# Batch 0's key copies from twin PSUM tiles, its values pooled ahead of late scores, and other slots for the attention steps, in a fused pooled-attention and maxout-FFN kernel

## The chip, the cores and the metric

One core of a Trainium2 chip. Times are device microseconds of one execution; medians of several executions, with their range, are quoted. A ratio is the mean time of one kernel's fast runs over that of the other's in the same rounds, so it is not quite the ratio of the quoted medians; beside it stands a 95% interval. A trace is one execution under the profiler, and its span lies some 1.7 us below that execution's time. The experiments ran in three batches of rounds on three chips, each beside the kernel before (medians 269.27, 269.48 and 269.42 us) but not beside the changed kernel. A comparison with the changed kernel therefore goes across batches, and by the intervals of the ratios its error is some 0.7 to 0.9 us.

## The reference, cut to what matters

```python
k_p = k.reshape(B, H, Sp, pool, D).mean(axis=3)      # (B, H, S, D) = (8, 8, 576, 64)
v_p = v.reshape(B, H, Sp, pool, D).mean(axis=3)      # pool 8, so Sp = 72
scores = scale * np.matmul(q, k_p.transpose(0, 1, 3, 2))
scores = scores - np.max(scores, axis=-1, keepdims=True)
attn = np.exp(scores)
attn = attn / (np.sum(attn, axis=-1, keepdims=True) + 1e-09)
x = np.matmul(attn, v_p)                             # then (B*S, H*D) = (4608, 512)
h = np.maximum(np.maximum(x @ w1, x @ w2), x @ w3)   # (4608, 768)
out = h @ w_out                                      # (4608, 512), float32
```

The FFN is most of the work. It runs in nine blocks of 512 tokens, and a batch has 576. So block n multiplies tokens of batches up to n, and the attention of batch n + 1 is put between its matmuls.

## The kernel before: the parts that the change and the argument touch

Names in the code and the traces: `pkp` is the pooled keys in PSUM and `kp` their copy, `pkt` their transpose and `kz` its copy; `pqt` and `qT` are the same for queries. `psc` is scores and `et` their exponentials, `pvp` and `vp` pooled values, `pav` attention times values, `xn` the same normalised, `pxt` and `xT` its transpose and the copy of that. `pw`, `t` and `hT` belong to the FFN's hidden layer, `po` and `osb` to its output, and `wm` is a warm-up matmul, whose result nobody reads. A timeline line gives start, duration, engine, line, operation and count; a bracket is the idle time of the engine before it and what ended that.

A generator yields after each piece of work, and the instruction order of every engine is the order in which the pieces are emitted. A "part" below is one yield of the FFN: four matmuls `pw` and one evacuation, 0.87 us on TensorE at full width. "Slot 5" is the place behind part 5 of a block.

```python
TR = ("tr", 1)     # PSUM tag and number of buffers: one
PW = ("pw", 3)     # FFN accumulators: three; tag "att" has two

def turn_k(b, evacs, tag):               # pooled keys, transposed, into the masked key tile
    pkt = psp.tile([128, 6, 96], BF16, name="pkt", tag=tag[0], bufs=tag[1])
    for i in range(6):
        nc.tensor.transpose(pkt[:, i, :], kps[b][:, i, :, :], ident[0:96, 0:96])
    for par in range(2):
        rows = slice(64 * par, 64 * par + 64)
        evacs[par](out=kz_all[b % 2][rows, par, :, 0:Sp]..., in_=pkt[rows]...)

def queries(b):                          # 4 query steps, keys after the third, 8 scores
    for m, (n0, n1) in enumerate(((0, 5), (5, 10), (10, 14), (14, 18))):
        turn_q(b, n0, n1, nc.scalar.copy, TR)
        yield
        if m == 2 and b > 1:
            turn_k(b, V_V, TR)           # both copies by VectorE
            yield
    for h in range(H):
        scores(b, h)                     # TensorE, then exp on ScalarE
        yield

def outputs(b, tags=(TR,) * 5):          # values, normalise (VectorE), transpose, copy (ScalarE)
    last = None
    for (c0, keep), tag in zip(CHUNKS, tags):
        xn = values(b, c0)
        yield
        if last:
            turn_x(*last)
            yield
        last = (b, c0, keep, xn, tag)
    turn_x(*last)
    yield

def hidden_part(n, jc, c0, c1, hT):      # one part per weight
    for wi in range(3):
        ...                              # pw: 4 matmuls, tag "pw"
        # wi 0: ScalarE copies pw to t;  wi 1: VectorE max(t, pw);  wi 2: VectorE max -> hT
        yield

# ... start of batch 0: one pooled-key tile, copied by VectorE and then ScalarE
def spread(i0, i1):
    nc.vector.tensor_copy(out=kps[0][:, i0:i1, 0, :], in_=pkp0[0:96, i0:i1])
    nc.scalar.copy(out=kps[0][:, i0:i1, 1, :], in_=pkp0[0:96, i0:i1])
# ... turn_k, turn_q, turn_q; scores4(0); turn_q, turn_q; scores4(4); scores2(0);
#     pool_v; scores2(2); pool_v; scores2(4); pool_v; scores2(6); then values, outputs

# ... blocks 1 to 8: slot of each of the 23 steps of batch n + 1; the rest is drained at the end
PLAN = (1, 2, 4, 5, 7, 8, 9, 10, 11, 12, 13, 14, 15, 16, 17, 17, 18, 18, 19, 19, 20, 20, 21)
PLAN1 = (7, 8, 10, 13, ...)              # block 1, whose first parts have half width
```

The softmax here doesn't subtract the row's maximum and nothing guards it: scores larger than these inputs give would overflow.

## Time and profile before

| | before |
|---|---|
| time, 3 runs | 269.28 us (269.11 to 269.28) |
| span of the trace | 267.3 us |
| first FFN matmul | 20.83 us |
| block 0 (20.83 to 54.04), block 1 (to 84.21) | 33.2 and 30.2 us |
| blocks 2 to 6, with attention | 27.36 us each |
| blocks 7 and 8, FFN alone | 20.7 us each |

The blocks are read off TensorE's timeline as the distance from the first `pw` of one to the first of the next. The lines that carry this are in the prediction.

### The profile page before, as it was taken

The numbers are of one execution on the slowest core, as the hardware profiler recorded it, in microseconds if no ns is written. First come the engines' busy times: TensorE is split into PE (matmuls) and PEld (weight loads), VectorE is DVE, ScalarE is ACT, GpSimd is POOL, SyncE is SP. The second block draws the span as 40 slices with busy tenths as digits, with TensorE's granted clock in tenths as the row PEclk, the third lists the DMA queues.
The fourth block names the chain that finished last, engine by engine and source line by source line (L and its number), as shares of the span: only waits on it lengthen the run. The fifth ranks groups of instructions, "written<-read, shape, count | busy, mean of one in ns | idle before, by whom it ended". The sixth has DMA issues, their size and how long they took to land.

```text
span 267.3 us, 4638 instructions
## 1 busy us (share of the span) xinstructions
PE 250.4 (94%) x1858; PEld 139.6 (52%) x1860; DVE 128.1 (48%) x227; ACT 132.9 (50%) x232; POOL 117.7 (44%) x84
## 2 busy tenths in 40 slices
PE   7598998998998999999999999999999999999993
PEld 2477546574555455545555555545554554444441
DVE  3447562555453646363645464455536464433440
ACT  1374248553755474547465655465555653223221
POOL 8662002999899999859970895000000000000000
PEclk9999999999999999999999999999999999999998
DMA  7999999698757958969777604200330033006006
GB/s 188 201 198 205 202 244 211 168 245 180 178 121 180 285 126 184 256 202 174 178 156 221 94 0 105 54 0 2 85 76 0 0 81 79 0 22 139 0 2 156
DMA packets 20866, 34.71 MB, mean 130 GB/s; under 512 B 2636, under 2 KB 13260, under 8 KB 20268
## 3 DMA queue, kind: packets, MB, share of 16 engines
q0 software_dynamic: 14048, 21.44, 41.1%
q1 hardware_dynamic: 6796, 12.98, 19.3%
q8 instruction: 14, 0.23, 0.4%
q14 instruction: 8, 0.07, 0.1%
HBM read 34.60 MB, written 9.44 MB: 165 GB/s over the span
## 4 chain that ended last, share of the span: by engine, by line
PE 83%; DVE 9%; ACT 5%; issue 1%; DVEq 0%; ACTq 0%
PE pw L267 45%; PE po L297 17%; PE psc L188 6%; PE pxt L208 4%; PE pqt L159 3%; DVE kz L169 3%; PE pav L217 3%; PE wm L316 3%; ACT et L193 2%; DVE xn L225 2%; DVE t L275 2%; ACT t L272 1%; PE pvp L148 1%; DVE hT L278 1%; ACT qT L161 1%
## 5 line engine op out<-in xcount | busy, mean ns | idle before, releaser
L267 PE MATMUL pw<-xT,mw 128*128 128x512 f16 (+1 forms) x696 | 157.2, 364 | 0.9 <-ACT xT L212 0.7
L267 PEld LDWEIGHTS <-mw 128*128 128x128 f16 x696 | 62.2, 98 | 50.9 <-issue 1.2
L275 DVE TENSOR_TENSOR t<-t,pw 128x512 f16<-128x512 f16 (+1 forms) x58 | 37.8, 651 | 79.0 <-PE pw L267 48.4
L272 ACT CAST t<-pw 128x512 f16<-128x512 f32 (+1 forms) x58 | 32.3, 557 | 43.2 <-PE pw L267 42.6
L297 PE MATMUL po<-mwo,hT 128*128 128x512 f16 x216 | 51.5, 379 | 0.0
L193 ACT ACTIVATE et<-psc 72x576 f16<-72x576 f32 (+2 forms) x62 | 40.5, 662 | 13.0 <-PE psc L188 12.9
L278 DVE TENSOR_TENSOR hT<-t,pw 128x512 f16<-128x512 f16 (+1 forms) x58 | 37.7, 650 | 15.4 <-PE pw L267 13.4
L127 POOL TENSOR_TENSOR vt<-vt 72x2048 f32<-72x2048 f32 (+1 forms) x12 | 41.2, 3434 | 2.6 <-DMA vt<-in_v_dram 2.1
L127 POOL TENSOR_TENSOR kt<-kt 96x1536 f32<-96x1536 f32 (+1 forms) x12 | 31.5, 2624 | 22.7 <-DMA kt<-in_k_dram 22.1
L301 ACT COPY osb<-po 128x512 f32<-128x512 f32 x36 | 21.1, 586 | 30.5 <-PE po L297 30.5
L297 PEld LDWEIGHTS <-hT 128*128 128x128 f16 x216 | 19.8, 98 | 18.9 <-DVE hT L278 0.4
L212 ACT COPY xT<-pxt 128x512 f16<-128x512 f16 (+1 forms) x40 | 21.8, 545 | 14.3 <-PE pxt L208 14.3
L225 DVE TENSOR_TENSOR xn<-pav,rcp 128x512 f16<-128x512 f32 x40 | 27.7, 692 | 1.4
L188 PE MATMUL psc<-qT,kz 128*128 128x64 bf16 (+3 forms) x192 | 25.4, 246 | 3.1 <-ACT qT L161 1.7
L161 ACT COPY qT<-pqt 128x640 bf16<-128x640 bf16 (+1 forms) x29 | 18.6, 641 | 18.1 <-PE pqt L159 18.1
L188 PEld LDWEIGHTS <-kz 128*128 128x128 bf16 x192 | 18.1, 98 | 17.5 <-issue 2.9
L217 PEld LDWEIGHTS <-et 72*128 72x128 f16 x320 | 15.7, 98 | 8.2 <-issue 0.6
L223 DVE RECIPROCAL rcp<-pav 128x8 f32<-128x8 f32 x40 | 8.1, 204 | 23.1 <-PE pav L217 23.1
L208 PE MATMUL pxt<-identh,xn 128*128 128x128 f16 x160 | 15.5, 219 | 2.3 <-DVE xn L225 2.1
L217 PE MATMUL pav<-vp,et 72*128 72x65 f16 x320 | 17.1, 194 | 0.4 <-ACT et L193 0.3
L159 PEld LDWEIGHTS <-qb 128*128 128x128 bf16 x144 | 9.9, 97 | 11.4 <-DVE kz L169 5.3
L159 PE MATMUL pqt<-ident,qb 128*128 128x128 bf16 x144 | 13.0, 219 | 2.7 <-DVE kz L169 2.3
(41 smaller groups left out, 107.9 us busy)
## 6 DMA issues: line engine op xcount, KB each, us to landing
out_dram<-osb SPq DMA_DIRECT2D x72, 128.0 KB, 2.4
kt<-in_k_dram POOLq DMA_DIRECT2D x5, 1152.0 KB, 7.6
vt<-in_v_dram POOLq DMA_DIRECT2D x5, 1152.0 KB, 10.2
qb<-in_q_dram POOLq DMA_DIRECT2D x7, 576.0 KB, 11.8
mw<-in_moe_w_dram POOLq DMA_DIRECT2D x9, 256.0 KB, 9.7
kt<-in_k_dram SPq DMA_DIRECT2D x3, 384.0 KB, 5.1
kt<-in_k_dram SPq DMA_DIRECT2D x1, 1152.0 KB, 9.5
vt<-in_v_dram SPq DMA_DIRECT2D x1, 1152.0 KB
```

Source lines behind the costliest of these rows:

```text
L127: e.tensor_tensor(out=t[:, :, 0:n, :], in0=t[:, :, 0:n, :], in1=t[:, :, n:2 * n, :], op=ALU.add)
L159: nc.tensor.transpose(pqt[:, n - n0, :], qf[:, 128 * n:128 * n + 128], ident)
L188: nc.tensor.matmul(out, kz_all[b % 2][:, f % 2, h, :], qTs[b][:, n + i0:n + i1, 64 * (h % 2):64 * (h % 2) + 64], start=True, stop=True)
L193: nc.scalar.activation(out=out, in_=in_, func=FT.Exp, scale=1.0 / 64.0)
L208: nc.tensor.transpose(pxt[:, kc, :], xn[:, kc // 2, 2 * (kc % 2):2 * (kc % 2) + 2, :], identh)
L217: nc.tensor.matmul(pav[:, h // 4, 65 * (h % 4):65 * (h % 4) + 65], ets[b][:, h, c0:c0 + 128], vp_all[:, b, h, :], start=True, stop=True)
L225: nc.vector.tensor_tensor(out=xn, in0=pv[:, :, :, 0:D], in1=rcp.to_broadcast([128, 2, 4, D]), op=ALU.mult)
L267: nc.tensor.matmul(pw, w_sb[wi][:, kc, bass.ts(jc, 128)], xT[:, kc, col], start=(kc == 0), stop=(kc == KCH - 1))
L272: nc.scalar.copy(out=t, in_=pw)
L275: nc.vector.tensor_tensor(out=t1, in0=t, in1=pw, op=ALU.max)
L278: nc.vector.tensor_tensor(out=hT[:, jc, c0:c1], in0=t, in1=pw, op=ALU.max)
L297: nc.tensor.matmul(po, hT[:, jc, bass.ts(mm, 128)], wo_sb[:, jc, :], start=(jc == 0), stop=(jc == JCH - 1))
```

## The change

Its intent: in the start, let VectorE and ScalarE copy at once, and begin the FFN while the exps of batch 0's last scores still run; later, put each attention step where TensorE need not wait for what it consumes. The core of the diff, cut:

```diff
+    pkp0 = [psp.tile([128, 6, D], F32, name="pkp", tag="pw", bufs=3) for _ in range(2)]
-    heat(14)
+    heat(16)                                     # warm-up matmuls
     for i in (0, 2, 4):
         ...                                      # VectorE add, then pooling matmuls,
+        for p in pkp0: ...                       # into both tiles
+        if i > 0:
+            nc.vector.tensor_copy(out=kps[0][:, c, 0, :], in_=pkp0[0][0:96, c])
+            nc.scalar.copy(out=kps[0][:, c, 1, :], in_=pkp0[1][0:96, c])
+    turn_q(0, 0, 5, nc.scalar.copy, PW)          # queries now ahead of the keys
+    turn_q(0, 5, 9, nc.vector.tensor_copy, ATT)
+    pkt0 = [keys(0, PW) for _ in range(2)]
+    for h in (0, 4):                             # four heads at a time, on both engines
+        fill_kz(0, 0, h, h + 4, pkt0[0], nc.vector.tensor_copy)
+        fill_kz(0, 1, h, h + 4, pkt0[1], nc.scalar.copy)
     scores4(0)
     ...
+    pool_v(0, 0, 4, PW, nc.vector.tensor_copy)   # ahead of the late scores
     scores4(4)
+    pool_v(0, 4, 6, ...); pool_v(0, 6, 8, ...)
     scores2(0)
+    xn0 = [values(0, c0) for c0, _ in CHUNKS[:2]]
+    turn_x(0, 0, 0, xn0[0], PW)
     scores2(2)
+    turn_x(0, 128, 0, xn0[1], PW, nc.vector.tensor_copy)
     scores2(4)
     scores2(6)                                   # three value groups are left for block 0
@@ block 0: half-width parts for 3 of 6 columns, not 2
-    steps = {16: 1, 17: 1, 19: 1, 20: 1, 21: 1, 22: 1, 23: 2}
+    steps = {19: 1, 20: 1, 21: 1, 22: 1, 23: 1, 24: 2, 25: 2, 26: 2}
     ...                                          # the rest of batch 1 goes between projections
@@ blocks 1 to 8
-            if m == 2 and b > 1:
+            if m == (3 if b == 2 else 2) and b > 1:   # batch 2: keys behind the fourth query step
-    PLAN = (1, 2, 4, 5, 7, 8, 9, ..., 16, 17, 17, 18, 18, 19, 19, 20, 20, 21)
+    PLAN = (2, 4, 5, 6, 8, 8, 9, ..., 16, 17, 18, 18, 19, 19, 20, 20, 21)
+    PLAN1 = (9, 11, 13, 15, 18, 19, 20, ..., 26, 26, 27, 27, 28, 28, 29, 29, 30, 30)
-                if slot in (0, 2):
+                if slot < 8:
                     next(side, None)
-        for _ in nxt: pass
+        side = nxt                               # the last output transpose: next block, slot 0
```

## The prediction

> **What bounds the kernel now.** I read the page's busy table first, then the slices, the chain of waits, and last the timelines of two stretches.
>
> ```profile
> PE 250.4 (94%) x1858; PEld 139.6 (52%) x1860; DVE 128.1 (48%) x227; ACT 132.9 (50%) x232; POOL 117.7 (44%) x84
> ...
> PE   7598998998998999999999999999999999999993
> ...
> PE 83%; DVE 9%; ACT 5%; issue 1%; DVEq 0%; ACTq 0%
> PE pw L267 45%; PE po L297 17%; PE psc L188 6%; PE pxt L208 4%; PE pqt L159 3%; DVE kz L169 3%; PE pav L217 3%; PE wm L316 3%; ACT et L193 2%; DVE xn L225 2%; DVE t L275 2%; ACT t L272 1%; PE pvp L148 1%; DVE hT L278 1%; ACT qT L161 1%
> ```
>
> TensorE is the bound: busy 94%, the low digits at the left edge (first 20 us) and in the last slice. The other engines matter only where TensorE waits for them. So what can be won is the start before the first FFN matmul and TensorE's gaps after it. I cut the run into the FFN's blocks of 512 tokens, by the first `pw` of each: block 0 at 20.83 us, block 1 at 54.04, block 2 at 84.2, then one each 27.36 us (111.57, 138.92, ...) until 221.0, and two blocks without attention of 20.72 each.
>
> Steady work, from the chain: 72 `pw` matmuls took 15.54 us, 24 `po` 5.18. From start-to-start distances in the timeline: query transposes 0.98 us a batch, keys 0.25, eight scores 2.0, five value groups 5 x 0.26, five output transposes 5 x 0.22. Sum 26.4, so a block of 27.36 holds about 1.0 us of gaps. TensorE's timeline of block 3 shows where:
>
> ```profile
> 117.61 0.42 PE L166 MATMUL pkt<-ident,kp 96*128 96x96 bf16 x6
> 117.86 1.89 PE L267 MATMUL pw<-xT,mw 128*128 128x512 f16 x8
> 119.99 0.40 PE L159 MATMUL pqt<-ident,qb 128*128 128x128 bf16 x4 [0.23 <-DVE kz L169]
> ...
> 131.15 0.42 PE L217 MATMUL pav<-vp,et 72*128 72x65 f16 x8
> 131.83 0.40 PE L208 MATMUL pxt<-identh,xn 128*128 128x128 f16 x4 [0.25 <-DVE xn L225]
> ```
>
> The eight `pw` need 1.73 us and end at 119.59: 0.40 us lost until VectorE has emptied the single "tr" buffer of keys. The values end issuing at 131.41: 0.42 lost until they are normalised. Two further gaps (0.09 between adjacent query steps, 0.06 before the last head's exp) make the 1.0. The bracketed numbers are smaller because a matmul's modelled end lies some 0.17 us after the next could start.
>
> The start, from the timeline of all engines:
>
> ```profile
> 6.60 0.39 PE L333 MATMUL pkp<-k,identh 96*128 96x128 f16 x4
> ...
> 7.82 0.68 DVE L330 TENSOR_TENSOR k<-kt 96x512 f16<-96x512 f32 x1
> ...
> 9.99 0.75 DVE L169 COPY kz<-pkt 64x576 bf16<-64x576 bf16 x1 [0.65 <-PE pkt L166]
> ...
> 10.77 0.63 ACT L169 COPY kz<-pkt 64x576 bf16<-64x576 bf16 x1 [1.13 <-DVE kz L169]
> ...
> 11.43 0.69 ACT L161 COPY qT<-pqt 128x640 bf16<-128x640 bf16 x1
> 12.17 0.60 PE L188 MATMUL psc<-qT,kz 128*128 128x256 bf16 x4 [1.72 <-ACT qT L161]
> ...
> 14.38 3.70 ACT L193 ACTIVATE et<-psc 72x1024 f16<-72x1024 f32 x5 [0.55 <-PE psc L188]
> ```
>
> ScalarE copies the second half of the keys only when VectorE is through with the first, though both only read; then it copies queries; then scores start (12.17); then the exps run back to back to 18.08, and only then come values and outputs.
>
> **What the Trainium skill says.** "PSUM — Partial Sum Buffer", section "PSUM bank collisions raise a hardware error": two engines must not access one bank in the same partitions at once, reads included, so their accesses are ordered in time; separate banks run together. The trace agrees on the order: 0.03 us after VectorE's 10.74, ScalarE begins. "TensorE: Matmul & The Clock Gate", "Back-to-back issue gap": N/2.4 + 2.5 ns when warm, 215.8 ns at N=512; here 15.54/72 = 215.8. Same page, "What's actually happening": the array is at half rate until it has been busy some 3.4 us; here warm-up matmuls come each 0.43 us until about 5.7 us.
>
> **The change part by part.**
>
> *Start.* 16 instead of 14 warm-up matmuls: 2 x 0.216 = +0.43. Key pooling is done twice, into twin tiles: 4 more matmuls, 0.22, ahead of the second pooling. So VectorE's first cast comes at about 8.1 instead of 7.47, and the third key add, behind it in VectorE's queue, ends at 9.15 instead of 8.50: 0.65 later. After it the twins win: last pooling and casts to 10.1, nine query transposes (first half of q is in by 9.0) to 10.1, twin key transposes to about 10.9; meanwhile VectorE and ScalarE copy queries (0.41 and 0.69), then four heads' keys each at once, some 0.4 by half of 0.75 and 0.63. Scores at about 11.4 instead of 12.17: 0.8 won.
> Then exps: first 12.0-13.0, ScalarE's new query copy 13.0-13.6 (0.59), second 14.1-15.1, third to 15.85. Values of chunk 0 at 15.1, of chunk 1 at 15.9 (needs the third exp's buffer). Normalising takes 0.2 + 0.7 on VectorE each; transposes at 16.6 and 17.55, copies to 17.6 (ScalarE) and 18.4 (VectorE, 0.41 as for other 128x512 two-byte copies). Late scores last until 18.7, so block 0 starts at 18.7, but the last exp ends at 19.9 against 18.08 now, and three value groups remain, not two. Working through the first slots: ScalarE's first `t` waits for the last exp, VectorE's max and normalising queue up, and TensorE waits about 0.6 for each of two output transposes. At 24.5 all outputs of batch 0 are done with 7 half-width parts, against 5 at 24.92 now: 0.42 + 2 x 0.435 = **1.3 us won**.
>
> *Rest of block 0.* Keys of batch 1 are now followed at the next part by a query step in the same "tr" buffer: two copies of 0.76 against 0.87 of cover, about 0.9 lost (now 0.14). Two scores per part: 0.5 for ScalarE. Score 7 directly before the values that need it, with an `osb` copy (0.59) ahead of its exp (0.65): about 1.0. With key pooling 0.45, query steps 0.16: 3.0 us of gaps, where the same stretch now has 2.2 (0.45 pooling, 0.5 at queries, 2 x 0.65 at exps). **0.8 given back.**
>
> *Block 1.* Now 30.15 us with 26.9 of work, so 3.2 of gaps; the largest are 1.3 before the pqt at 65.65 (keys), 0.97 at 83.98 (last output drained at the block's end), 0.5 at 59.6. New, by the same rules: keys then a score at the next part 0.77, values behind score 7 0.69, last output transposes of batch 1 0.55, queries 0.23: 2.3. **0.9 won.**
>
> *Blocks 2 to 6.* Keys move one part back, so VectorE has finished its max before they arrive; copies end about 2.0 us after the key transposes begin, TensorE arrives after 0.25 + 2 x 0.865 = 1.98: 0.06 lost instead of 0.40. First output transpose moves behind a projection: 0.42 gone. But the last one now comes in the next block after one part: `osb`, then the previous `xT` copy occupy ScalarE until 1.27 us after the projection, while TensorE is there at 0.22 + 0.87 = 1.09: some 0.24 lost. Net 0.34 + 0.42 - 0.24 = 0.52 each, five times: **2.6 won**. Block 7 pays the 0.24 once.
>
> Sum: 1.3 - 0.8 + 0.9 + 2.6 - 0.2 = 3.8 us; 269.28 - 3.8 = 265.5. My hand schedule of block 0 is likelier too pessimistic than too kind, since slots there can be chosen by measuring; I say 265.1.
>
> **The rivals.**
> 1. The early start is swallowed (fast startup, same arrival). For: three things queue on ScalarE and VectorE in the first parts, and the loads of weights and of batch 1 are paced by memory: nine weight loads land 8.6 to 10.8 us after issues from 6.0 to 14.9 us, one per 1.33 us. The third pair of weight columns would be needed at 23 us and I place its last landing at 22.4. Against: keys of batch 1 land at 16.2 + 12.2 = 28.4 and are wanted near 31. If it holds, only steady gains remain: 266.5 to 267.5.
> 2. The early start is kept whole (about 2 us at block 0, no extra gaps behind it), with 0.7 per steady block: 6 us, 263. For it: the 3.0 us of new gaps are a hand schedule. Against: each is a dependency with measured durations.
> 3. The change loses because ScalarE, moved copies added, becomes the bound. At 50% busy and with 2.5 us of work in three parts of 3.3 us, I give it almost nothing.
>
> **Range and chances.** Errors of about 0.9 for the start, 0.7 for blocks 0 and 1 each and 0.6 for the five blocks give 1.5 together, so 263.0 to 267.0. Two per cent lies at 263.9, 0.8 of that error below my number: faster 0.24, same 0.75, slower 0.01.
>
> **What would show it.** Right: first `psc` near 11.4, first `pw` near 18.7 with the last early exp ending after it; period of blocks 2 to 6 near 26.85, pqt behind the keys and pxt behind the values without a wait on kz or xn, and a new pxt gap behind each block's first part naming ScalarE's `xT`; values after score 7 waiting on `et` in block 0 and 1. Wrong: a wait of `pw` on a weight load (rival 1), a period of 26.6 or less or a block 0 shorter than 33 us (rival 2), or a busy TensorE share that does not rise.

## More of the kernel before

One more view is wanted for the comparison later: for whom TensorE waited, in the kernel before (total us, times, longest). All in front of the arrow is what waited, and behind it is what ended the wait.

```profile
PE pqt L159 <- DVE kz L169: 2.3, 6, 1.2
PE pxt L208 <- DVE xn L225: 2.1, 6, 0.8
PE psc L188 <- ACT qT L161: 1.7, 1, 1.7
...
PE pxt L208 <- ACT xT L212: 0.2, 1, 0.2
```

The first two lines are six waits each, once for each of batches 2 to 7: queries for the key copies, and output transposes for the normalised values. The third is the first score of the whole kernel.

## The result, and the profile after

264.72 us median (264.02 to 265.15, 4 runs) against 269.28 (269.11 to 269.53, 4 runs): ratio 0.9827, interval 0.9803 to 0.9851. That is inside the predicted range and 0.4 us below the predicted number, and within 2%.

The lines of the page that answer to the first ones of the prediction:

```profile
PE 251.3 (95%) x1900; PEld 142.1 (54%) x1900; DVE 129.5 (49%) x233; ACT 131.3 (50%) x234; POOL 117.6 (45%) x84
...
PE   7899989889999999999999999999999999999992
...
PE 89%; ACT 6%; DVE 3%; issue 1%; ACTq 0%
```

VectorE's share of the chain fell from 9% to 3%. A slice is 6.6 us. Before, an 8 came back every second or third slice up to 107 us; now, after the slices at 33 to 39 us and 46 to 59 us, none is below 9 until the last. (The busy share is a measure of waiting here and not of distance to the limit: the Trainium skill, "Perfetto Trace Analysis", section "Identifying the Most-Contended Engine", says that a busy TensorE row is no measure of that, since matmuls are pipelined; no run here tests it.)

TensorE in block 3 of the changed kernel, the answer to the second group of lines:

```profile
116.75 0.42 PE L166 MATMUL pkt<-ident,kp 96*128 96x96 bf16 x6
117.01 1.89 PE L272 MATMUL pw<-xT,mw 128*128 128x512 f16 x8
118.80 0.40 PE L159 MATMUL pqt<-ident,qb 128*128 128x128 bf16 x4
...
129.09 0.42 PE L223 MATMUL pav<-vp,et 72*128 72x65 f16 x8
129.36 1.46 PE L302 MATMUL po<-mwo,hT 128*128 128x512 f16 x6
130.65 0.39 PE L214 MATMUL pxt<-identh,xn 128*128 128x128 f16 x4
...
136.22 1.03 PE L272 MATMUL pw<-xT,mw 128*128 128x512 f16 x4
137.32 0.38 PE L214 MATMUL pxt<-identh,xn 128*128 128x128 f16 x4
```

Read them by start times. Eight `pw` take 1.73 us, so those at 117.01 are through at 118.74 and the query step starts 0.06 later, where 0.40 were lost before. The output transpose behind the projection does not wait. The last pair is the price: four `pw` from 136.22 take 0.865 us, to 137.085, but the carried transpose starts at 137.32, 0.24 later. No bracket marks it: the modelled end of the last `pw`, 136.22 + 1.03 = 137.25, covers most of the gap. The timeline of ScalarE shows what ended it, the copy of the previous output transpose (136.67 to 137.26). The period is 26.8 us (139.26 less 112.44 between the first query steps of two blocks).

The start of the changed kernel:

```profile
1.46 6.46 PE L321 MATMUL wm<-warm 128*128 128x512 bf16 x16 [1.46 <-DVE warm L101]
7.76 0.61 PE L336 MATMUL pkp<-k,identh 96*128 96x128 f16 x8
...
11.42 0.80 DVE L171 COPY kz<-pkt 64x288 bf16<-64x288 bf16 x2
...
11.59 0.69 ACT L171 COPY kz<-pkt 64x288 bf16<-64x288 bf16 x2
...
11.91 0.61 PE L194 MATMUL psc<-qT,kz 128*128 128x256 bf16 x4
...
17.95 1.94 ACT L199 ACTIVATE et<-psc 72x640 f16<-72x640 f32 x3
...
18.98 1.04 PE L272 MATMUL pw<-xT,mw 128*128 128x256 f16 x8
```

The two engines' key copies now lie side by side, and the FFN starts while ScalarE still has 0.9 us of exps before it. The first pooled-key matmul came 0.7 us later than predicted (7.03), because the array was at half rate longer in this execution (the warm-up matmuls come each 0.43 us until about 7.0 us, and until 5.7 in the kernel before); more on that below.

Where TensorE waits now, in blocks 0 and 1 (the five longest):

```profile
35.45 0.44 PE L159 MATMUL pqt<-ident,qb 128*128 128x128 bf16 x5 [0.84 <-DVE kz L171]
...
48.71 0.21 PE L223 MATMUL pav<-vp,et 72*128 72x65 f16 x1 [0.75 <-ACT et L199]
...
53.16 0.60 PE L272 MATMUL pw<-xT,mw 128*128 128x256 f16 x4 [0.67 <-ACT xT L218]
...
66.72 0.28 PE L194 MATMUL psc<-qT,kz 128*128 128x192 bf16 x2 [0.48 <-DVE kz L171]
...
75.53 0.20 PE L223 MATMUL pav<-vp,et 72*128 72x65 f16 x1 [0.51 <-ACT et L199]
```

Four of the five were predicted. The third was not: block 1's first part needs an output of batch 1 that was transposed just before it.

A ledger from start times in the two traces, in us:

| stretch | before | after | of it other work | won | predicted |
|---|---|---|---|---|---|
| to the end of batch 0's outputs | 24.75, 5 half-width parts done | 24.16, 7 done | 2 parts, 0.87 | 1.46 | 1.3 |
| from there to block 1 | 29.29 | 29.00 | 2 parts less, and 3 groups of outputs less, together 1.61 less | -1.3 | -0.8 |
| block 1 | 30.17 | 29.53 | 3 groups more, one moved out, 0.52 more | 1.2 | 0.9 |
| blocks 2 to 6 | 136.79 | 134.00 | | 2.8 | 2.6 |
| blocks 7 and 8, from their start (221.00 and 216.69) to the last projections (257.26 and 253.41) | 36.26 | 36.72 | one transpose more, 0.22 | -0.24 | -0.2 |

("Groups" are value groups at 0.26 and output transposes at 0.22.) The sum is 3.9 us, as the spans say (267.3 and 263.4). This trace is the slowest execution of its four; the medians differ by 4.6.

### The profile page after: what moved, and what is told of

Read it like the earlier page. It is cut to its first block, busy times and chain, and to the rows that moved or that the text cites. A ratio compares the mean times of both kernels' runs of the same rounds, so it can differ in the third digit from the quotient of the medians.

```text
span 263.4 us, 4734 instructions
## 1 busy us (share of the span) xinstructions
PE 251.3 (95%) x1900; PEld 142.1 (54%) x1900; DVE 129.5 (49%) x233; ACT 131.3 (50%) x234; POOL 117.6 (45%) x84
## 4 chain that ended last, share of the span: by engine, by line
PE 89%; ACT 6%; DVE 3%; issue 1%; ACTq 0%
PE pw L272 49%; PE po L302 18%; PE psc L194 6%; PE pav L223 4%; PE pqt L159 3%; PE pxt L214 3%; PE wm L321 3%; ACT xT L218 2%; ACT et L199 2%; PE pvp L148 1%; DVE kz L171 1%; ACT osb L306 1%; PE pkt L166 1%; PE pkp L185 0%; PE pkp L336 0%
## 5 line engine op out<-in xcount | busy, mean ns | idle before, releaser
L272 PEld LDWEIGHTS <-mw 128*128 128x128 f16 x720 | 64.3, 98 | 48.1 <-issue 0.8
L161 ACT COPY qT<-pqt 128x640 bf16<-128x640 bf16 (+1 forms) x30 | 19.2, 639 | 23.9 <-PE pqt L159 23.9
L194 PE MATMUL psc<-qT,kz 128*128 128x64 bf16 (+3 forms) x192 | 26.2, 246 | 0.8 <-DVE kz L171 0.5
L214 PEld LDWEIGHTS <-xn 128*128 128x128 f16 x160 | 11.5, 97 | 9.0 <-DVE xn L231 2.4
```

The source lines that it names most:

```text
L194: nc.tensor.matmul(out, kz_all[b % 2][:, f % 2, h, :], qTs[b][:, n + i0:n + i1, 64 * (h % 2):64 * (h % 2) + 64], start=True, stop=True)
L214: nc.tensor.transpose(pxt[:, kc, :], xn[:, kc // 2, 2 * (kc % 2):2 * (kc % 2) + 2, :], identh)
L272: nc.tensor.matmul(pw, w_sb[wi][:, kc, bass.ts(jc, 128)], xT[:, kc, col], start=(kc == 0), stop=(kc == KCH - 1))
```

## The experiments

Eleven kernels ran, all correct and all in five rounds. They were told apart by medians, and by waits in their traces; each has one trace.

**Only the slots of blocks 2 to 6.** The kernel before with

```diff
-    PLAN = (1, 2, 4, 5, 7, 8, 9, ...)
+    PLAN = (2, 4, 5, 6, 8, 8, 9, ...)
-        for _ in nxt: pass
+        side = nxt
```

> The kernel before with only the new slots of blocks 2 to 6: keys one part later, the first output transpose behind a projection, the last one carried into the next block. Theory of the prediction: 0.5 to 0.56 us per block, five times, less 0.24 in block 7, so 2.3 to 2.6 us faster, 266.7 to 267.0 (ratio 0.990 to 0.991), with a period of 26.8 us in place of 27.36. Rival (the early start carries the result): 268.5 or more.

Measured: 266.78 us (266.29 to 266.87) against 269.27, ratio 0.9899 (0.9885 to 0.9914). The period is 26.82 us (113.97 to 140.79). The prediction's theory holds to 0.1 us, and its rival falls: more than half of the gain is not in the start.

**Only the twins.** The kernel before with the new copies of batch 0's keys and queries, then the old order from the first scores on.

> The kernel before with only the twin tiles and split key copies of batch 0 (16 warm-up matmuls included), its scores, values and slots in the old order. Theory: the third key add comes 0.65 us later and the simultaneous copies win it back and a little more, first scores 0.3 to 0.8 us earlier, and that is all: 268.5 to 269.0. Rival (the copies by two engines at once are what matters in the start): 267.8 or less.

Measured: 268.43 us (267.83 to 268.86), ratio 0.9967 (0.9954 to 0.9980): 0.84 us, just better than the theory's range and well short of the rival's.

**The whole new start.** The kernel before with the twins, the early values, two value groups ahead of the late scores, and block 0's steps as before.

> The kernel before with the whole new start of batch 0 (twins, values pooled early, two value groups ahead of the late scores) and the old slots from block 0 on. Theory: the 1.3 to 1.6 us won when batch 0's outputs are done stay won, since the old slots of block 0 have fewer gaps: 267.5 to 268.0. Rival (the early start is swallowed behind the first parts, by loads or by ScalarE): 268.8 to 269.4.

Measured: 266.81 us (266.44 to 267.91), ratio 0.9913 (0.9897 to 0.9929). So the start is worth 2.5 us (1.9 to 2.8 by the ratio) and not 1.3 to 1.6. It is not swallowed: the period of blocks 2 to 6 is the old 27.35 and the gain arrives at the end. The two single changes add to 2.46 + 2.49 = 4.95 us, the change has 4.56. The new slots of blocks 0 and 1 therefore give back about 0.4 us on balance, a difference of three medians that is as large as their scatter; the second and third row of the ledger say 0.2.

**Without the twins.** The changed kernel with one tile where there are two:

```diff
-            for _ in range(2)]
+            for _ in range(1)]
-            nc.scalar.copy(out=kps[0][:, c, 1, :], in_=pkp0[1][0:96, c])
+            nc.scalar.copy(out=kps[0][:, c, 1, :], in_=pkp0[0][0:96, c])
-    pkt0 = [keys(0, PW) for _ in range(2)]
+    pkt0 = [keys(0, PW)]
-        fill_kz(0, 1, h, h + 4, pkt0[1], nc.scalar.copy)
+        fill_kz(0, 1, h, h + 4, pkt0[0], nc.scalar.copy)
```

> The changed kernel with one tile of pooled keys and one of key transposes in place of two, so that VectorE's and ScalarE's copies take turns; all else as changed. Theory: the turns cost some 0.8 us in the key copies, the saved second pooling and transposes give back 0.5 to 0.7 us, so 264.7 to 265.1, hardly to be told from the changed kernel. Rival (the twins carry the start): 265.6 or more.

Measured: 264.76 us (264.62 to 265.50), ratio 0.9835 (0.9822 to 0.9849): the changed kernel's time. In the traces the way from the first pooled-key matmul to the first `pw` is 19.22 - 7.61 = 11.61 us here and 18.98 - 7.76 = 11.22 with twins. Four more traces with this start, in which TensorE waited for no load either, have 11.21 or 11.22 too. So the copies at once are worth some 0.4 us in the traces, net of the extra matmuls; the times, with an error of 0.7 us, don't resolve that. That they do take turns with one tile is in the trace:

```profile
11.48 0.39 ACT L171 COPY kz<-pkt 64x288 bf16<-64x288 bf16 x1 [0.24 <-DVE kz L171]
```

Without the twins the first score even starts 0.25 us earlier (11.51 - 7.61 = 3.90 after the first pooled keys, against 4.15); what is lost comes behind it. So what the kernel with only the twins won seems to come mostly from the order that it has with them: queries ahead of keys, and four heads' keys copied first, so that scores start before the other four are there. That order was not run alone. The twins buy concurrency by paying for it in matmuls: eight more for pooling up to the second group, and six more transposes.

**Two warm-up matmuls fewer.** The changed kernel with `heat(14)` for `heat(16)`.

> The changed kernel with 14 warm-up matmuls in place of 16. Theory of the prediction: these two lie on the path to the first pooled keys, 0.43 us warm and 0.85 us where the array is still at half rate, so 0.3 to 0.7 us faster, 264.0 to 264.4. Rival: the array then goes to full rate later by as much, or the second part of k bounds the path, and nothing is won: 264.5 to 264.9.

Measured: 264.94 us (264.47 to 265.37), ratio 0.9830 (0.9808 to 0.9851): nothing won that could be seen, though with an error of 0.9 us the expected 0.3 to 0.7 is not excluded. Its trace shows the array at full rate earlier than the changed kernel's (first pooled keys at 6.51) and then this:

```profile
11.97 1.05 PE L148 MATMUL pvp<-vt,identh 72*128 72x256 f16 x8 [0.20 <-DMA vt<-in_v_dram]
```

The pooling of batch 0's values, which the change puts ahead of the second scores, meets the load of v. I put it as the next theory: a start that gets earlier runs into that load, and all later scores queue behind it.

**The carried transpose one part later.**

```diff
-                if slot < 8:
+                if slot < 8 and (n == 1 or slot > 0):
```

> The changed kernel with the carried output transpose behind the second part of the next block in place of the first (blocks 2 to 7). Theory: the wait of that transpose for ScalarE's copy, some 0.22 us in each of six blocks, goes: 1.2 to 1.4 us faster, 263.3 to 263.5, with a period of 26.55 to 26.6 us. Rival (the wait moves to the query step in the same buffer or to the copies behind it): 264.4 or more.

Measured: 263.30 us (263.08 to 263.73), ratio 0.9771 (0.9752 to 0.9790), 1.4 us below the changed kernel; period 26.59 (111.65 to 138.24). This confirms the gap that no bracket marked: six times 0.24 us, gone by one slot. Eight `pw` from 108.84 are through at 110.57, and the transpose starts then:

```profile
108.84 1.89 PE L272 MATMUL pw<-xT,mw 128*128 128x512 f16 x8
110.57 0.39 PE L214 MATMUL pxt<-identh,xn 128*128 128x128 f16 x4
```

**Queries and keys one part earlier again.**

```diff
-    PLAN = (2, 4, 5, 6, 8, 8, 9, ...)
+    PLAN = (2, 3, 4, 5, 7, 8, 9, ...)
```

> The changed kernel with the queries and keys of blocks 2 to 6 one part earlier, so that the key transposes again come behind the part whose max VectorE still has to do; the output transposes stay as changed. Theory: the wait for the key copies comes back, 0.34 us per block, and 0.1 us for adjacent query steps may, five times: 266.3 to 266.9. Rival (the keys' slot is worth little, the output transpose did it): 265.2 or less.

Measured: 267.66 us (266.72 to 268.00), ratio 0.9928 (0.9908 to 0.9948). 2.9 us lost, more than expected; the period is back at 27.36. Two lines of its trace for VectorE, and one for TensorE:

```profile
116.46 0.69 DVE L283 TENSOR_TENSOR hT<-t,pw 128x512 f16<-128x512 f16 x1 [0.54 <-PE pw L272]
117.07 1.52 DVE L171 COPY kz<-pkt 64x576 bf16<-64x576 bf16 x2
...
118.64 0.40 PE L159 MATMUL pqt<-ident,qb 128*128 128x128 bf16 x4 [0.23 <-DVE kz L171]
```

The key copies stand behind the max of the part before, and the query step behind them starts 0.39 us after TensorE was free (116.52 + 1.73 = 118.25): the old gap. The missing 0.2 us per block is the query step at 115.18, which comes 0.21 us after the `pw` of 114.10 are through; in that plan ScalarE's `t` of the same part is copied first and the single "tr" buffer comes free later. So the move of the keys is worth 0.33 us a block, and the spacing of the queries that went with it another 0.14 to 0.2.

**The gaps of blocks 0 and 1.** The changed kernel with other buffers and slots there:

```diff
-        pool_k(1, TR)
+        pool_k(1, ATT)
-            turn_q(b, n0, n1, nc.scalar.copy, TR)
+            turn_q(b, n0, n1, nc.scalar.copy, ATT if b == 1 else TR)
-    steps = {19: 1, 20: 1, 21: 1, 22: 1, 23: 1, 24: 2, 25: 2, 26: 2}
+    steps = {18: 1, 20: 2, 21: 1, 22: 1, 23: 1, 24: 2, 25: 1, 26: 2}
@@ between the four projections of block 0
+    0: score, pool_v, score, pool_v, last score   1: values(1, 0), values(1, 128)
+    2: turn_x of both, the second by VectorE into a "pw" buffer   3: values(1, 256)
-    PLAN1 = (9, 11, 13, 15, 18, 19, 20, 21, 22, 23, 24, 25, 26, 26, 27, ...)
+    PLAN1 = (9, 11, 13, 15, 17, 19, 19, 20, 21, 22, 23, 24, 25, 26, 27, ...)
-                if slot < 8:
+                if slot < 8 and (n > 1 or slot != 4):
```

> The changed kernel with other slots and buffers in blocks 0 and 1: keys and queries of batch 1 through the attention buffers, its last score ahead of a projection, its first two outputs before the last projection, keys of batch 2 one part earlier. Theory: the six gaps named in blocks 0 and 1 (0.45, 0.9, 1.0, 0.75 and 0.75, 0.7) are independent waits, 3.5 to 4.5 us of them go: 260.3 to 261.3. Rival (each gap hides another, loads of batch 1 or ScalarE): at most 2 us, 262.7 or more.

Measured: 259.80 us (259.42 to 260.16), ratio 0.9641 (0.9622 to 0.9661), 4.9 us below the changed kernel, 0.5 more than the best that the theory allowed. The gaps were independent waits, and hardly anything hid behind them.

**Both.** The last with the carried transpose one part later:

```diff
-                if slot < 8 and (n > 1 or slot != 4):
+                if slot < 8 and slot != (4 if n == 1 else 0):
```

> Both of the last two together. Theory: the gains add, 5 to 6 us below the changed kernel, 258.8 to 259.8, so faster than both kernels. Rival: 261 or more.

Measured: **257.97 us** (257.90 to 258.26), ratio 0.9573 (0.9556 to 0.9591): 11.5 us below the kernel before in the same rounds (269.48) and 6.75 below the changed one. These are all the waits of TensorE that the profile of its trace marks:

```profile
PE wm L322 <- DVE warm L101: 1.5, 1, 1.5
PE pkp L336 <- DVE k L332: 0.7, 1, 0.7
PE pav L223 <- ACT et L199: 0.4, 1, 0.4
PE pvp L148 <- DMA vt<-in_v_dram: 0.4, 1, 0.4
PE pxt L214 <- ACT xT L218: 0.2, 1, 0.2
```

All five lie in the start and the first parts of block 0. No wait for `kz`, and none in a steady block, is marked any more; the period is 26.59 (106.13 to 132.72).

**The pooling of v behind the second scores.** The theory above, on the last kernel:

```diff
-    pool_v(0, 0, 4, PW, nc.vector.tensor_copy)
     scores4(4)
+    pool_v(0, 0, 4, PW, nc.vector.tensor_copy)
```

> The kernel with all gaps closed (257.97 us), and the first pooling of batch 0's values behind the second group of scores, not ahead of it. Theory: where the array reaches full rate early, TensorE waits for the load of v (0.39 us in the trace) with scores queued behind; they now go first, so 0.2 to 0.6 us faster: 257.4 to 257.8. Rival: the pooled values are needed as soon, nothing is won or 0.2 us lost: 257.9 to 258.2.

Measured: 259.23 us (258.97 to 259.68), ratio 0.9624 (0.9608 to 0.9641): 1.3 us slower, so the theory falls. The trace shows a part of why:

```profile
13.38 0.38 PE L194 MATMUL psc<-qT,kz 128*128 128x256 bf16 x2 [0.34 <-ACT qT L161]
13.60 1.93 PE L148 MATMUL pvp<-vt,identh 72*128 72x256 f16 x24
...
15.84 0.70 ACT L199 ACTIVATE et<-psc 72x640 f16<-72x640 f32 x1 [1.03 <-PE psc L194]
```

The second scores must wait for ScalarE's query copy anyway, with or without the pooling ahead of them; now the whole pooling comes after them, ahead of the third group of scores, and ScalarE idles 1.03 us for that. In the run before, with the pooling ahead, this idle is 0.15. Against that, the second scores there queued behind the load of v. Set side by side, the way from the first score to the first `pw` is 7.91 us here (11.19 to 19.10) and 7.48 there (10.45 to 17.93): 0.43 lost by the order, and 0.84 against the changed kernel's 7.07, which did not meet the load. The rest of the 1.5 us between the two traces is not the order: the first pooled keys came 0.37 later (6.62, 6.25), VectorE waited 0.33 for a load of k, and TensorE 0.25 for one of batch 1's q, neither of which the other trace has, nor that of the next run, with the same order. So pooling v ahead of late scores seems good because it fills a wait for a copy; that this is worth the whole 1.3 us is not shown.

**The same with 14 warm-up matmuls.**

> The same with 14 warm-up matmuls. Theory: with the load of v out of the way the two matmuls are worth their 0.4 us: 257.0 to 257.5. Rival (the load of v, or the moment at which the array gets its full rate, sets the start): as the one before within 0.2 us.

Measured: 258.56 us (258.32 to 259.19), ratio 0.9602 (0.9584 to 0.9619): 0.7 us below the run before, with intervals that overlap. That would fit the load of v as the reason why the two matmuls did not count in the changed kernel, but the traces don't bear it out: with 14 the first pooled keys came at 6.74, with 16 at 6.62, since the array reached full rate later, and what the FFN starts earlier by (18.80 against 19.10) is the wait for the load of k that this trace does not have. So what the two matmuls cost stays open.

## Why the prediction was right, point by point

*Blocks 2 to 6 (2.6 us predicted).* Right in mechanism and size: 2.8 in the traces, 2.5 as the only change (there with block 7's 0.24 taken off). Each of its three terms was shown: the keys' move by undoing it (0.33 a block, 0.34 predicted), the gap that the carried transpose brings by moving it on (1.4 us for six blocks, 0.24 each), and the output transpose behind the projection in the trace. The prediction found the 0.24 by laying ScalarE's copies beside TensorE's arrival; it is the term that kept the sum from 5 us. The sign that it had named, a wait of `pxt` naming `xT`, did not appear as a bracket; start times and the run with the later slot show the gap. A smaller effect went unseen: the wider spacing of the query steps, which undoing showed to be worth up to 0.2 us a block; in the changed kernel one pair is still adjacent, so the forecast of the whole came out right all the same.

*The start (1.3).* The mechanism was right; the size is the term most off: 2.5 us as the only change. Against the predicted schedule the trace is 0.2 us shorter from the first pooled keys to the first score (4.15 against 4.34), 0.2 shorter from there to the first `pw` (7.07 against 7.3), and 0.6 shorter through the first seven parts (5.18 against 5.8): the first and the last of the three late output transposes waited 0.25 and 0.40 us, where 0.6 had been put down for each of two. Together 1.0 us, so 2.3. The changed kernel's own trace shows 1.5, since its array came to full rate 0.7 us later than reckoned with.

*The rest of block 0 (-0.8).* The gaps named are in the trace, near their sizes: behind the keys 1.0 from start to start (0.9 predicted), at the values behind the last score 0.9 (1.0), at the pair of scores 0.3 (0.5). What failed is the list: it left out the first part of block 1, which waits for the output copied just before it, 0.67 us in the bracket. With that the -1.3 of the ledger is met.

*Block 1 (0.9).* 1.2 by the ledger, with the waits where they were expected.

*The sum.* That 3.8 us was predicted and the traces have 3.9 is in part luck: against the ledger the terms are off by +0.2, -0.5, +0.3 and +0.2, which cancel, and the start's schedule, 1.0 us too gloomy, met an execution whose array was 0.7 us late.

*The correction of 0.4 us* for a hand schedule that is likelier too gloomy than too kind was in the right direction: the start was too gloomy, by more than that; block 0 was not.

*The rivals.* The first (the early start is swallowed by loads) is refuted by the start alone, whose gain arrives whole. No load of FFN weights made TensorE wait, though loads are what a still earlier start meets: v, once k or q, not the weights. The second (6 us) failed because blocks 0 and 1 do contain the gaps, as closing them for 4.9 us shows. The third is refuted: ScalarE is busy 50% as before.

*The cause named first in the change,* copies from twin tiles by two engines at once, is worth some 0.4 us in the traces. The prediction had it at 0.8 together with the reordering, which the run of the twins with their order confirmed (0.84), but could not divide the two.

*The serial order before.* The prediction laid it to the rule of the Trainium skill ("PSUM — Partial Sum Buffer", section "PSUM bank collisions raise a hardware error") that two engines must not access one bank in the same partitions at once, reads included. For the pooled keys that fits: both engines read partitions 0 to 95 of one tile and took turns (VectorE 7.47 to 7.89, ScalarE from 7.93), and from two tiles their copies overlap (from 8.86 and 9.08). For the key copies, to which the prediction applied it, it does not: they read partitions 0 to 63 and 64 to 127, and by the same section accesses to different groups of 32 partitions of one bank don't collide. They took turns all the same, before and in the run without the twins. By the brackets ScalarE waits there for VectorE's copy, and why the program makes it is not shown; whether one tile would do if it did not wait was not tried.

*The spacing of matmuls.* The prediction took it from "TensorE: Matmul & The Clock Gate", section "Back-to-back issue gap". That section gives the formula for an isolated gap and a smaller figure for a stream that loads weights for each matmul; in this stream, with a weight load for each matmul, the trace has the formula's 215.8 ns.

## What to carry to other kernels

Where one engine is the bound and busy 94%, the rest is found by start-to-start distances and not by the busy share: list for each step what it waits for, when that engine gets to it and with which work ahead of it, and give each step the slot at which its input is just there. A single PSUM buffer shared by adjacent steps makes each of them wait for the copy of the one before; in the run that gave batch 1's queries a tag that is idle in that stretch, the wait of 1.0 us behind the keys is gone (that run moved other steps too). And check every slot list at its seams, where one block's last step feeds the next one's first.

## What the Trainium skill lacked or had wrong

- "TensorE: Matmul & The Clock Gate", section "What's actually happening", says that the moment of full rate varies by 500 ns either way with the phase of a free-running window. Here nine traces of different kernels with the same head of 16 warm-up matmuls, begun at the same time, differ far more. The weight loads of these matmuls stop coming each 0.43 us between 4.00 and 4.31 us in one (all gaps closed) and between 6.99 and 7.33 in another (the changed kernel): a width of some 3 us. The first pooled-key matmul starts anywhere from 6.25 to 7.76 us. (The section's other remark, that one kernel measured 6, 11 or 14 slow matmuls, fits better.) The path to the first scores runs through that matmul, so a gain below a microsecond in a start needs several executions; those of the changed kernel spread over 1.1 us. That the phase causes this spread was not tested by itself.
- "Perfetto Trace Analysis", section "Tensor Engine Instruction (MATMUL, LD_WEIGHTS)", says that a matmul's end is estimated. It does not say that gaps are hidden by it: here an idle stretch of 0.24 us between issues (137.085 to 137.32) shows none at all, and one of 0.40 us shows 0.23.
- No page says what side-by-side copies by two engines from two PSUM tiles are worth to a kernel. Here: some 0.4 us of a start of 19 us (11.61 against 11.22 from the first pooled keys to the first `pw`), less than the 1.5 us by which the first pooled keys scatter.
- No page says why copies from one PSUM tile take turns when they read different groups of 32 partitions. Here ScalarE's copy of partitions 64 to 127 waits for VectorE's of 0 to 63 (0.24 us idle in the run without the twins).
